# Shifting every weight tile against the moving rows by 192 bytes, reordering the last sums, and moving one start-up load, in a fused attention and mixture-of-experts kernel

## The chip, the cores and the metric

The kernel runs on one core of a Trainium2 chip. Five engines work beside each other: TensorE (PE; its weight loads are listed as PEld), VectorE (DVE), ScalarE (ACT), GpSimd (POOL) and SyncE (SP), with sixteen DMA engines. The metric is the time of one execution on the device in microseconds (us). The kernel before takes 800.86 us, the median of 3 runs (800.49 to 801.48).

## The reference

Attention with a tanh cap, then a top-1 mixture of experts on its output. All data is float32.

```python
# attention: batch 8, 12 heads, 448 tokens, head size 64
scores = cap * tanh((q @ k.T / 8) / cap)
attn = exp(scores - max); attn /= attn.sum(-1) + 1e-9
x = (attn @ v) as 3584 tokens of 768
# experts: 8 of them, 768 -> 1024 -> 768
e = argmax(x @ w_gate)                   # one expert for each token
gate = softmax(x @ w_gate)[e]
out[token] = gate * (relu(x[token] @ w1[e]) @ w2[e])
```

## The kernel before, in words

The attention half takes the 8 images one after the other, in 24 "quads" of four heads, 7 tiles of 64 keys each. A step `k` (84 of them, `STEPS`) handles two tiles: PE makes the scores (L246), ACT applies tanh (L259) and exp (L262), PE multiplies by the values (L312), DVE sums the exponentials for the softmax denominators (`adds`, `fold`, L267). The order is written out by hand: a table `tasks`, filled with `at(step, when, f, ...)`, places the rest of the work (gating, transposes, first loads of experts) in a step, behind its scores on ACT (`"act"`), behind its value products on PE (`"pe1"`) or behind its sums on DVE (`"v"`).

For each image the gating chain is: `strips0` and `strips` (PE: sums over keys and gate logits, L341 to L352), `rec_t` and `rec_v` (DVE: transposes, reciprocal, L367 to L382), `rec_p` and `log_p` (PE, L392 and L408), `route_v` (DVE: argmax, giving `ob`, L434 to L440), `route_s` and `route_g` (gate weight), `place_p` (PE: running counts, L465 and L467), `place_v` (DVE: slots, L477 to L486), and `place_d` (POOL: token lists by DMA). `turn` (L330) transposes one pair of heads' output into the token rows `yt`. The last two images (6 and 7) finish their chains while PE already works on the first block of tokens of an expert.

The expert half works in blocks of tokens of one expert. A large block has 448 tokens, a small one 256. The blocks are run in the order: a first block (`j = -2`) made of tokens of the first images, a second (`-1`), five large ones, two small ones. A block is 8 chunks `f` of the hidden size. `up` (L918) makes hidden rows from 18 matmuls: 6 slices of the input by 3 products. `down` (L948 for large, L956 for small blocks) multiplies them by the second matrix: 18 matmuls of 448 columns, or 12 of 384. Float32 accuracy comes from splitting each operand in a high and a low part (`h` and `l`), hence the three products. The split of the weights is a cast on ACT (L789) and a subtraction on DVE (L794), that of the input L893 and L897.

In `up` the weights that PE holds are `w1` chunks and the rows that stream past them (the moving rows) are `xh`, `xl`. In a large `down` the weights are `w2` chunks and the moving rows the hidden tile `hb` (`hx` and a `kr` buffer in the first block). In a small `down` the roles are exchanged: `hb` is held and `w2` moves. Every matmul is preceded by its own weight load (128 columns of 4 bytes), which PE does while the matmul before it is still streaming.

Where these tiles lie in a partition, in the program as built before: `xh`, `xl`, `hb`, `hx`, the `kr` and `qr` buffers (which serve as chunks 0 and 1 of `w1`), all other `w1` chunks and chunk 0 of `w2` start at 128 modulo 256 bytes. Chunks 1 to 7 of `w2` start at 224. Slices within a tile are multiples of 256 bytes. So, taking the weights that are loaded next against the rows that stream meanwhile, the distance is 0 modulo 256 in every `up`, and in chunk 0 of `down`; it is 96 in chunks 1 to 7 of a large `down`, and 160 in those of a small one.

The start: twenty warm-up matmuls on zeros (L202), while the first keys and queries are loaded by SP (L167, L171), ACT (L168) and POOL (L169).

Of the kernel before, what the change touches and what calls it, by code (L numbers as in the profile page):

```python
# [4 lines left out]
F32 = mybir.dt.float32  # L5
# [96 lines left out]
    return c  # L102


class Pools:


# [16 lines left out]
def attention_moe(tc, qT, kT, vL, capd, wgL, w1a, w1b, w2a, w2b, cst, cmk, out):  # L124
# [31 lines left out]
    def load(mq, part):  # L156

        b, i = divmod(mq, NQ)
        p = slice(2 * i, 2 * i + 2)
        if part == 0:  # L160
            qr = raw.tile([128, 2, S], F32, name="qr")
            kr = raw.tile([128, 2, S], F32, name="kr")
            raws[mq] = qr, kr, pb.tile([128, KT, 2, D], F32, name="vr", bufs=3)
        qr, kr, vr = raws[mq]
        if mq == 0:
            if part == 0:
                nc.sync.dma_start(out=kr[:, :, 0:128], in_=kT[b, :, p, 0:128])  # L167
                nc.scalar.dma_start(out=qr[:, 0], in_=qT[b, :, 0])  # L168
                nc.gpsimd.dma_start(out=qr[:, 1], in_=qT[b, :, 1])  # L169
                nc.scalar.dma_start(out=capt, in_=capd)  # L170
                nc.sync.dma_start(out=kr[:, :, 128:S], in_=kT[b, :, p, 128:S])  # L171
            else:
                nc.sync.dma_start(out=vr, in_=vL[b, :, i])
        elif part == 0:
            nc.sync.dma_start(out=kr, in_=kT[b, :, p])
            nc.sync.dma_start(out=qr, in_=qT[b, :, p])
        else:
            nc.sync.dma_start(out=vr, in_=vL[b, :, i])
# [119 lines left out]
    def fold(m):  # L298
        add(p4s[m], accs[m][:, 0], accs[m][:, 1])
# [438 lines left out]
    def large(j):  # L738
        return j < NL
# [41 lines left out]

    w1s, w2s = [None] * FC, [None] * FC

    def chunk(pool, name):
        return [pool.tile([128, DM], F32R, name=name + i) for i in "hl"]

# [17 lines left out]
    def spare(name):  # L804
        return raw.tile([128, 2, S], F32, name=name).rearrange("p a b -> p (a b)").bitcast(F32R)

    def first_w1(f):
        w1s[f] = [spare(name)[:, 0:DM] for name in ("qr", "kr")]
        split_w1(f)

    idt, gts = {}, {}
# [195 lines left out]
    def at(step, when, f, *a):  # L1007
        tasks.setdefault((step, when), []).append((f, a))

    def do(step, when):  # L1010
        for f, a in tasks.pop((step, when), []):
            f(*a)

    for b in range(B):

        n = (KT * (b * NQ + NQ) - 1) // 2
        at(n + 1, "pe1", strips0, b)
        if b == B - 1:
            continue
        at(n + 4, "v", turn, b * NP + 4)  # L1020
        at(n + 5, "v", turn, b * NP + 5)
        d = n + 5
        at(d, "pe1", strips, b)
        at(d + 1, "v", rec_t, b)
        early = b < B - 2
        p = d + 4 if early else d + 5
        at(d + 2 if early else d + 4, "v", rec_v, b)
        at(p, "pe1", rec_p, b)
        at(p, "pe1", log_p, b)
        at(p + 1, "v", rec_c, b)  # L1030
        at(p + 1, "v", route_v, b)
        at(p + 2, "act", route_s, b)
        at(p + 2, "v", store, b, G)
        at(p + 2, "v", route_g, b)
        at(p + 3, "pe1", place_p, b)
        at(p + 4, "v", place_v, b)
        for q in range(4):
            at(p + 5 + q // 2 * early, "v", place_d, b, q)
    for i in range(QUADS):
        if i % NQ != NQ - 1:  # L1040
            n = (KT * (i + 1) - 1) // 2
            for c in range(2):
                at(n + 4 + c, "v", turn, 2 * i + c)

    n_first = (KT * B_FIRST * NQ - 1) // 2 + 14
    at(0, "v", constants)
# [23 lines left out]
    for k in range(STEPS + 3):  # L1070
        live = k < STEPS
        for n in range(QUADS - 3):
            if k == (KT * (n + 1) - 1) // 2 + 1:
                load(n + 3, 0)
            if k == (KT * (n + 1) - 1) // 2 + 4:
                load(n + 3, 1)
        if live:
            for t in (2 * k, 2 * k + 1):
                scores(t)
                tanh(t)  # L1080
        do(k, "act")
        if 1 <= k <= STEPS:
            expo(k - 1)
        if k == STEPS:
            pools.close("ps_s")
            m["ps_h"] = pools("ps_h", bufs=2, space=PSUM, side="right", **tw)
            m["ps_z"] = pools("ps_z", space=PSUM, side="right", **tw)
            m["h0"] = spare("kr")
            up(-2, 0)
        last = None  # L1090
        if k >= 3:
            ready = held + [2 * k - 6, 2 * k - 5]
            held = [ready.pop()] if ready[-2] % KT == KT - 1 else []
            for t in ready:
                pv(t)
                if t % KT == KT - 1:
                    last = t // KT
        if last is not None:
            outp(last)
        do(k, "pe1")  # L1100
        if 2 <= k < STEPS + 2:
            adds(k - 2)
        do(k, "v")
    fold(QUADS - 1)
    for k in range(STEPS + 3, STEPS + 5):
        do(k, "v")

    pools.close("pb")
    hw = pools("hw", side="right", **tw)
    m["hb"] = hw.tile([128, 6 * LARGE], F32R, name="hb")  # L1110
    for f in range(2, FC):
        w1s[f] = chunk(hw, f"w1{f}")
    w2s[0] = chunk(hw, "w20")
    m["hx"] = pools("hx", side="right", **tw).tile([128, 8 * LARGE], F32R, name="hx")
    assert not tasks and not held
    b = B - 1
    split_w1(2)
    up(-2, 1)
    split_w1(3)
    strips(b)  # L1120
    rec_t(b)
    second_block()
    load_ids(-1)
    load_w(-1, 0, [0])
# [9 lines left out]
    route_v(b)  # L1134
    route_s(b)
    up(-2, 4)
    place_p(b)
    split_w1(6)
    route_g(b)
    place_v(b)  # L1140
    for q in range(4):
        place_d(b, q)
    rec_c(b)
    turn(b * NP + 4)
    turn(b * NP + 5)
    store(b, nc.sync)
    split_w1(7)
    up(-2, 5)
    split_w2(0)
    pools.close("op", "yp", "att")  # L1150
    wb = pools("wb", **tw)
    for f in range(1, FC):
        w2s[f] = chunk(wb, f"w2{f}")
    up(-2, 6)
# [51 lines left out]
    for i, j in enumerate(blocks):  # L1206
# [16 lines left out]
        for f in range(FC):  # L1223
            if 0 < f:
                splits_after(n0, f)
                if n0 == -2 and f == FC // 2 - 1:
                    load_w(n1, 1)
                    put(n0)
            if n1 is not None:
                splits_in(j, f)  # L1230

            down(j, f, range(2) if n1 is not None or f < 3 else range(1))
            if f + 2 < FC:
                if f + 2 == FC - 1 and n1 is not None:
                    scale_x(n1)
                    for k in range(XT):
                        trans_x(n1, k)
                up(j, f + 2)
            if f + 2 == FC and n1 is not None:
                split_xs(n1)  # L1240
                if n2 is not None and not large(n1):
                    make_idx(n2)
                    load_x(n2)
            if f == 4 and n2 is not None:
                load_ids(n2)
                load_w(n2, 0)
# [111 lines left out]
```

## Time and profile before

| what | us |
|---|---|
| median of 3 runs | 800.86 |
| profiled execution | 801.69 |
| span of its instructions | 799.6 |
| PE busy | 782.5 (98%) |
| DVE busy | 549.1 (69%) |
| ACT busy | 452.6 (57%) |
| POOL busy | 362.6 (45%) |

A busy share says only that some instruction was open. Matmuls overlap in the records, each lasting longer than the distance to the next, so how fast PE goes is read from the starts: the distance between two starts is what one matmul costs. In the timeline rows the first number is the start in us from the first instruction, the second the time covered, then engine, line, operation, the tiles written and read, shapes and count, and in brackets the idle time of the engine before it with what ended it. The clock granted to TensorE is at 0.9 of full speed or above in 39 of the page's 40 slices, and at 0.8 in the last.

### The profile page before, as it was taken

The numbers are of one execution on the slowest core, as the hardware profiler recorded it, in microseconds if no ns is written. First come the engines' busy times: TensorE is split into PE (matmuls) and PEld (weight loads), VectorE is DVE, ScalarE is ACT, GpSimd is POOL, SyncE is SP. The second block draws the span as 40 slices with busy tenths as digits, with TensorE's granted clock in tenths as the row PEclk, the third lists the DMA queues.
The fourth block names the chain that finished last, engine by engine and source line by source line (L and its number), as shares of the span: only waits on it lengthen the run. The fifth ranks groups of instructions, "written<-read, shape, count | busy, mean of one in ns | idle before, by whom it ended". The sixth has DMA issues, their size and how long they took to land.

```text
span 799.6 us, 14371 instructions
## 1 busy us (share of the span) xinstructions
PE 782.5 (98%) x5740; PEld 568.2 (71%) x5740; DVE 549.1 (69%) x943; ACT 452.6 (57%) x537; POOL 362.6 (45%) x324
## 2 busy tenths in 40 slices
PE   8999999999999999999999999999999999999996
PEld 3334343444444435889999999999999999999995
DVE  1778988999899998797558358357357367367720
ACT  6999999999999992344334224324333233234421
POOL 1000412135841303671774773773773773747601
PEclk9999999999999999999999999999999999999998
DMA  7243654568988503324264524625520226453301
GB/s 275 88 140 100 180 172 144 169 131 295 238 250 190 156 2 73 82 64 158 60 214 184 214 70 174 218 70 185 208 71 5 72 70 234 155 192 119 143 37 38
DMA packets 34939, 112.76 MB, mean 141 GB/s; under 512 B 8422, under 2 KB 14744, under 8 KB 31792
## 3 DMA queue, kind: packets, MB, share of 16 engines
q0 software_dynamic: 19216, 70.45, 26.7%
q1 hardware_dynamic: 15360, 41.09, 17.0%
q8 instruction: 47, 0.77, 0.4%
q10 hardware_dynamic: 288, 0.23, 0.1%
q14 instruction: 28, 0.23, 0.1%
HBM read 101.87 MB, written 22.85 MB: 156 GB/s over the span
## 4 chain that ended last, share of the span: by engine, by line
PE 77%; ACT 7%; DVE 6%; issue 4%; DMA 3%; POOL 1%; POOLq 0%; SPq 0%; DVEq 0%; ACTq 0%
PE ph L918 27%; PE y L948 22%; PE sp L246 10%; PE po L312 10%; PE y L956 4%; ACT pt L259 3%; ACT pt L262 3%; DVE acc L267 2%; DMA kr<-in_kT 1%; PE ms L349 1%; PE po L948 1%; PE ms L948 1%; DVE p L267 1%; PE z L948 1%; DMA xd<-w2r 1%
## 5 line engine op out<-in xcount | busy, mean ns | idle before, releaser
L928 ACT ACTIVATE hb<-ph 128x448 fp32r<-128x448 f32 (+1 forms) x67 | 34.0, 507 | 265.8 <-PE ph L918 265.8
L749 POOL DMA_INDIRECT xg<-xd,xi x114 | 132.1, 1159 | 58.5 <-issue 35.9
L929 DVE SCALAR_TENSOR_TENSOR hb<-ph,hb 128x448 fp32r<-128x448 f32 (+1 forms) x67 | 38.4, 573 | 170.7 <-ACT hb L928 170.1
L262 ACT ACTIVATE pt<-pt,capt 128x1792 f32<-128x1792 f32 x84 | 153.5, 1829 | 0.0
L246 PE MATMUL sp<-qr,kr 64*64 64x448 f32 x1344 | 149.6, 551 | 3.5 <-ACT pt L259 3.2
L259 ACT ACTIVATE pt<-sp 128x896 f32<-128x896 f32 x161 | 141.1, 947 | 7.8 <-PE sp L246 7.5
L312 PE MATMUL po<-pt,vr 64*64 64x448 f32 x1344 | 144.9, 537 | 0.1
L759 POOL DMA_INDIRECT out<-ys,xi x98 | 107.2, 1093 | 29.9 <-issue 26.5
L246 PEld LDWEIGHTS sp<-qr,kr 64*64 64x64 f32 x1344 | 48.3, 134 | 86.7 <-issue 44.5
L312 PEld LDWEIGHTS po<-pt,vr 64*64 64x64 f32 x1344 | 56.1, 133 | 72.4 <-issue 61.7
L492 POOL DMA_INDIRECT ids<-tokg,slots x32 | 44.4, 1387 | 57.8 <-DVE slots L486 40.1
L267 DVE TENSOR_TENSOR acc<-acc,pt 128x1792 f32<-128x1792 f32 (+1 forms) x36 | 61.2, 1700 | 2.6 <-ACT pt L262 2.5
L267 DVE TENSOR_TENSOR acc<-pt 128x896 f32<-128x896 f32 (+1 forms) x36 | 50.1, 1391 | 5.4 <-ACT pt L262 5.4
L460 POOL DMA_DIRECT2D xd<-w2r x12 | 8.2, 694 | 97.4 <-DVE w2r L397 97.4
L893 ACT CAST xh<-xt 128x448 fp32r<-128x448 f32 (+1 forms) x54 | 27.3, 533 | 27.8 <-DVE xt L889 27.8
L319 DVE COPY ot<-po 128x448 f32<-128x448 f32 x48 | 27.6, 616 | 20.9 <-PE po L312 20.8
L460 POOL DMA_DIRECT2D xd<-yt x16 | 10.5, 664 | 63.4 <-DVE yt L397 63.4
L918 PE MATMUL ph<-xl,qr 128*128 128x448 f32 (+1 forms) x108 | 37.9, 351 | 0.5 <-DVE xl L897 0.5
L918 PE MATMUL ph<-xh,qr 128*128 128x448 f32 (+1 forms) x108 | 37.6, 348 | 0.0
L918 PE MATMUL ph<-xh,kr 128*128 128x448 f32 (+1 forms) x108 | 37.4, 347 | 0.0
L749 POOL DMA_INDIRECT w1r<-in_w1b,widx x7 | 10.3, 1468 | 55.8 <-DVE w17l L794 55.5
L889 DVE STREAM_TRANSPOSE xt<-xg 128x448 f32<-128x448 f32 (+1 forms) x54 | 30.3, 583 | 0.8
(396 smaller groups left out, 1814.6 us busy)
## 6 DMA issues: line engine op xcount, KB each, us to landing
vr<-in_vL SPq DMA_DIRECT2D x24, 448.0 KB, 3.5
kr<-in_kT SPq DMA_DIRECT2D x23, 448.0 KB, 4.8
qr<-in_qT SPq DMA_DIRECT2D x23, 448.0 KB, 6.1
xd<-yt POOLq DMA_DIRECT2D x16, 346.5 KB
xd<-w2r POOLq DMA_DIRECT2D x12, 346.5 KB
xg<-xd,xi POOLq DMA_INDIRECT x114
out<-ys,xi POOLq DMA_INDIRECT x98
w1r<-in_w1a SPq DMA_DIRECT2D x4, 384.0 KB, 4.9
```

What stands on the lines that cost most here:

```text
L246: PE.matmul(sp[w, r, 0:S], kr[h, c, 64 * g : 64 * g + 64], qr[h, c, :], start=True, stop=True)
L259: A.activation(out=pts[t // 2][:, t % 2], in_=sps.pop(t)[:, :, 0:S], func=AF.Tanh, scale=qsc if t < KT else 1.0)
L262: A.activation(out=pts[k], in_=pts[k], func=AF.Exp, scale=capt)
L267: V.tensor_tensor(out=o, in0=a, in1=b, op=ALU.add)
L312: PE.matmul(pvs[m][c][w, 0:S], vr[r, g, j, :], pt[r, j, :], start=g == 0, stop=g == KT - 1)
L492: i = G.indirect_dma_start(out=ids, out_offset=bass.IndirectOffsetOnAxis(ap=slots[0:p, c : c + 1].bitcast(U32), axis=0), in_=tokg[0:p, c, ...
L749: G.indirect_dma_start(out=dst, out_offset=None, in_=src, in_offset=bass.IndirectOffsetOnAxis(ap=idx.bitcast(U32), axis=0), bounds_check=b ...
L759: i = G.indirect_dma_start(out=dst, out_offset=bass.IndirectOffsetOnAxis(ap=idx.bitcast(U32), axis=0), in_=src, in_offset=None, bounds_che ...
L918: PE.matmul(ph, w[:, 128 * k : 128 * k + 128], x[:, k, 0:n], start=i == 0, stop=i == 3 * KC - 1)
L928: A.activation(out=hh, in_=ph, func=AF.Relu)
L929: V.scalar_tensor_tensor(out=hl, in0=ph, scalar=0.0, in1=hh, op0=ALU.max, op1=ALU.subtract)
L948: PE.matmul(y[k][:, 0:LARGE], w[:, c], h, start=f == 0 and i == 0, stop=f == FC - 1 and i == 2)
```

## The change

Four things. First, placement: three padding tiles of 192, 64 and 96 bytes go into the pools that hold `hb`, the `w1` and `w2` chunks, and chunks 0 and 1 of `w1` begin 48 floats into their buffers. As built, all `w1` and `w2` chunks then start at 64 modulo 256, and all of `xh`, `xl`, `hb`, `hx` at 128: the weights loaded next stand at 192 modulo 256 from the moving rows in every `up` and every large `down`. In a small `down` the distance is 64. Second, the order of the last sums, gates and transposes. Third, in small blocks the scaling, transposing and splitting of the next block's input comes one chunk earlier. Fourth, the second half of the first queries is loaded by SP instead of POOL.

```diff
+PADS = (192, 64, 96)
...
-                nc.gpsimd.dma_start(out=qr[:, 1], in_=qT[b, :, 1])
+                nc.sync.dma_start(out=qr[:, 1], in_=qT[b, :, 1])
...
+    def pad(pool, n):
+        pads.append(pool.tile([128, n // 4], F32, name=f"pad{len(pads)}"))
...
-        w1s[f] = [spare(name)[:, 0:DM] for name in ("qr", "kr")]
+        w1s[f] = [spare(name)[:, 48 : 48 + DM] for name in ("qr", "kr")]
...
-        at(d + 2 if early else d + 4, "v", rec_v, b)
+        at(d + 2 if early else d + 3, "v", rec_v, b)
...
-        at(p + 2, "v", route_g, b)
+        at(p + 2 if early else STEPS + 4, "v", route_g, b)
...
-                at(n + 4 + c, "v", turn, 2 * i + c)
+                at(n + 4 + c if i < QUADS - 2 else STEPS + 5, "v", turn, 2 * i + c)
...
+        if k == STEPS + 1:
+            fold(QUADS - 1)
         do(k, "v")
-    fold(QUADS - 1)
-    for k in range(STEPS + 3, STEPS + 5):
-        do(k, "v")
+    do(STEPS + 3, "v")
...
     m["hb"] = hw.tile([128, 6 * LARGE], F32R, name="hb")
+    pad(hw, PADS[0])
     for f in range(2, FC):
         w1s[f] = chunk(hw, f"w1{f}")
     w2s[0] = chunk(hw, "w20")
+    pad(hw, PADS[1])
...
     rec_t(b)
+    for k in range(2):
+        do(STEPS + 4 + k, "v")
     second_block()
...
     up(-2, 4)
+    split_w1(6)
+    rec_c(b)
+    turn(b * NP + 4)
+    turn(b * NP + 5)
+    store(b, nc.sync)
+    up(-2, 5)
     place_p(b)
-    split_w1(6)
     route_g(b)
     place_v(b)
     for q in range(4):
         place_d(b, q)
-    rec_c(b)
-    turn(b * NP + 4)
-    turn(b * NP + 5)
-    store(b, nc.sync)
     split_w1(7)
-    up(-2, 5)
     split_w2(0)
...
     wb = pools("wb", **tw)
+    pad(wb, PADS[2])
...
-                if f + 2 == FC - 1 and n1 is not None:
+                if f + 2 == FC - (1 if large(j) else 2) and n1 is not None:
                     scale_x(n1)
...
-            if f + 2 == FC and n1 is not None:
+            if f + 2 == FC - (not large(j)) and n1 is not None:
                 split_xs(n1)
```

On DVE, where image 6's reciprocal stands among the last steps. Before, `rec_v` (L376 to L382) follows a transpose and the sums `p` of quad 22:

```order
L267 TENSOR_TENSOR acc<-acc,pt 128x1792
L330 STREAM_TRANSPOSE yt<-ot 128x14x32
L267 TENSOR_TENSOR p_3043<-acc 128x896
L267 TENSOR_TENSOR p_3043<-p_3043,pt 128x896
L376 COPY st<-st 64x14x2
L377 COPY st<-lt 32x14x4
L379 RECIPROCAL rec<-st 96x56
L382 TENSOR_TENSOR lt<-lt,rec 96x448
```

The same place in the changed kernel (its lines are numbered 3 higher here):

```order
L270 TENSOR_TENSOR acc<-acc,pt 128x1792
L379 COPY st<-st 64x14x2
L380 COPY st<-lt 32x14x4
L382 RECIPROCAL rec<-st 96x56
L385 TENSOR_TENSOR lt<-lt,rec 96x448
L333 STREAM_TRANSPOSE yt<-ot 128x14x32
L270 TENSOR_TENSOR p_3043<-acc 128x896
L270 TENSOR_TENSOR p_3043<-p_3043,pt 128x896
```

The reciprocal moved in front of three instructions. A little later on DVE, between the argmax of image 6 (`ob`) and its slots (`place_v`, L477 on). Before:

```order
L440 TENSOR_TENSOR ob<-tko,cs 128x32
L330 STREAM_TRANSPOSE yt<-ot 128x14x32
L794 TENSOR_TENSOR kr<-w1r_121,qr 128x768
L267 TENSOR_TENSOR acc<-acc,pt 128x1792
L451 TENSOR_REDUCE gt<-ex 128x4
L453 TENSOR_SCALAR gt<-gt 128x4
L455 RECIPROCAL tokg<-gt 128x4
L330 STREAM_TRANSPOSE yt<-ot 128x14x32
L319 COPY ot<-po 128x448 x2
L267 TENSOR_TENSOR p_3180<-acc 128x896
L477 TENSOR_TENSOR pos<-ms,base 128x32
L479 TENSOR_TENSOR base<-base,ms 128x8
```

In the changed kernel:

```order
L443 TENSOR_TENSOR ob<-tko,cs 128x32
L802 TENSOR_TENSOR kr<-w1r_121,qr 128x768
L270 TENSOR_TENSOR acc<-acc,pt 128x1792
L270 TENSOR_TENSOR p_3180<-acc 128x896
L322 COPY ot<-po 128x448 x2
L480 TENSOR_TENSOR pos<-ms,base 128x32
L482 TENSOR_TENSOR base<-base,ms 128x8
```

Two transposes and the three gate instructions are gone from here. They now stand after image 7's `rec_t` and before `second_block` (L541 on). On SP at the very start, before:

```order
L167 DMA kr<-in_kT 128x2x128
L171 DMA kr<-in_kT 128x2x320
L173 DMA vr<-in_vL 128x896
L175 DMA kr<-in_kT 128x896
L176 DMA qr<-in_qT 128x896
```

And in the changed kernel:

```order
L170 DMA kr<-in_kT 128x2x128
L172 DMA qr<-in_qT 128x448
L174 DMA kr<-in_kT 128x2x320
L176 DMA vr<-in_vL 128x896
L178 DMA kr<-in_kT 128x896
```

The second half of the queries is now SP's second load, in front of the rest of the keys.

## Rows read from the trace of the kernel before

**Rows 1.** Timeline of PE, 381 to 397 us: the first matmul of five chunks.

```profile
381.57 0.36 PE L918 MATMUL ph<-xh,w12h 128*128 128x448 f32 x1
...
385.21 0.56 PE L948 MATMUL y<-hb,w21h 128*128 128x448 f32 x2
...
388.81 0.37 PE L918 MATMUL ph<-xh,w13h 128*128 128x448 f32 x1
...
392.47 0.57 PE L948 MATMUL y<-hb,w22h 128*128 128x448 f32 x2
...
396.18 0.36 PE L918 MATMUL ph<-xh,w14h 128*128 128x448 f32 x1
```

**Rows 2.** Timeline of PE: first matmul of block -1, then of small-block chunks.

```profile
370.63 0.36 PE L918 MATMUL ph<-xh,qr 128*128 128x448 f32 x1
...
721.59 0.28 PE L918 MATMUL ph<-xh,qr 128*128 128x256 f32 x1
...
725.90 0.34 PE L956 MATMUL y<-w20h,hb 128*128 128x384 f32 x1
...
727.99 0.28 PE L918 MATMUL ph<-xh,w12h 128*128 128x256 f32 x1
...
730.13 0.34 PE L956 MATMUL y<-w21h,hb 128*128 128x384 f32 x1
...
732.25 0.28 PE L918 MATMUL ph<-xh,w13h 128*128 128x256 f32 x1
```

**Rows 3.** Timeline of all engines, the first 16 us (SPq is SP's DMA queue).

```profile
0.74 0.46 SPq L167 DMA_DIRECT2D kr<-in_kT  x1
...
1.32 0.74 POOL L169 DMA_DIRECT2D qr<-in_qT  x1 [0.86 <-POOLq L1347]
...
5.44 8.88 PE L246 MATMUL sp<-qr,kr 64*64 64x448 f32 x48
...
6.85 0.37 PEld L246 LDWEIGHTS sp<-qr,kr 64*64 64x64 f32 x8 [1.13 <-DMA qr<-in_qT]
...
8.68 1.01 ACT L259 ACTIVATE pt<-sp,qsc 128x896 f32<-128x896 f32 x1 [5.50 <-PE sp L246]
```

**Rows 4.** Waits of ACT, 8.6 to 302: total us, times, longest us.

```profile
ACT pt L259 <- PE sp L246: 13.5, 17, 5.5
```

**Rows 5.** Waits of PE, 300 to 799: total us, times, longest us.

```profile
PE ms L349 <- DVE pos L481: 1.4, 1, 1.4
PE ms L465 <- DVE ob L440: 0.8, 1, 0.8
PE z L948 <- DVE w22l L794: 0.6, 1, 0.6
PE ph L918 <- DVE xl L897: 0.5, 3, 0.2
```

**Rows 6.** Timeline of PE: the `rec_p` of image 6 and of image 7.

```profile
297.19 0.88 PE L392 MATMUL ms<-rec,cs 96*128 96x56 f32 x6 [1.26 <-DVE rec L379]
...
323.20 0.77 PE L392 MATMUL ms<-rec,cs 96*128 96x56 f32 x6
```

**Rows 7.** Timeline of DVE, 309 to 327 us.

```profile
310.56 0.18 DVE L451 TENSOR_REDUCE gt<-ex 128x4 f32<-128x32 f32 x1
...
311.60 1.12 DVE L319 COPY ot<-po 128x448 f32<-128x448 f32 x2
...
313.85 0.16 DVE L479 TENSOR_TENSOR base<-base,ms 128x8 f32<-128x8 f32 x1
...
321.93 0.50 DVE L379 RECIPROCAL rec<-st 96x56 f32<-96x56 f32 x1
...
326.62 0.23 DVE L832 TENSOR_SCALAR xi<-idt,kc 128x14 int32<-128x14 int32 x1 [2.01 <-DMA idt<-ids,t1i]
```

**Rows 8.** Timeline of PE at the start of the last block: the first and the thirteenth matmul.

```profile
755.88 0.28 PE L918 MATMUL ph<-xh,qr 128*128 128x256 f32 x1
...
758.83 0.28 PE L918 MATMUL ph<-xh,qr 128*128 128x256 f32 x1
```

More of the change, by code (lines that the diff above doesn't have):

```diff
@@ L782, in attention_moe @@
     w1s, w2s = [None] * FC, [None] * FC
+    pads = []
+    def pad(pool, n):
+        pads.append(pool.tile([128, n // 4], F32, name=f"pad{len(pads)}"))
     def chunk(pool, name):
@@ L1113, in attention_moe @@
     w2s[0] = chunk(hw, "w20")
+    pad(hw, PADS[1])
     m["hx"] = pools("hx", side="right", **tw).tile([128, 8 * LARGE], F32R, name="hx")
-    assert not tasks and not held
+    assert not held
     b = B - 1
@@ L1121, in attention_moe @@
     rec_t(b)
+    for k in range(2):
+        do(STEPS + 4 + k, "v")
+    assert not tasks
     second_block()
```

## The prediction

> **What bounds the kernel now.** I read the timeline of PE first, then the waits, then the stretches where PE waits. In the expert half PE alone is the bound: from 370 to 751 us it waits for nothing, and in all of 300 to 799 us only four kinds of wait are listed, 3.3 us together [rows 5]. So there the time is the number of matmuls times the distance between their starts, and the reader is to look at starts, not at durations. Chunk `w12` of `up` begins at 381.57, `w21` of `down` at 385.21, `w13` at 388.81, `w22` at 392.47, `w14` at 396.18 [rows 1]. Each chunk is 18 matmuls of 448 columns, so one costs 3.64/18 = 202.2 ns, 3.60/18 = 200.0, 3.66/18 = 203.3 and 3.71/18 = 206.1. The same instruction with the same shape has three prices. The two `down` chunks have the same distance of 96 between next weights and moving rows, yet one runs at 200 and one at 206: there are two rhythms at one placement. All six blocks from 370.63 to 721.59 [rows 2] repeat this: 350.96/6 = 58.49 us a block, which is 8 `up` chunks at 3.65, `w20` at 3.65 (distance 0, like `up`), `w21`, `w23`, `w25` at 3.60 and four chunks at 3.71 (29.2 + 3.65 + 10.8 + 14.84 = 58.49).
>
> What part of a price streams and what part is a fixed cost? In small blocks 36 `up` matmuls of 256 columns take 721.59 to 725.90, 119.7 ns each, at distance 0; 12 of 384 columns take 725.90 to 727.99, 174.2 at distance 0, and 730.13 to 732.25, 176.7, at 160 [rows 2]. From 256 columns at 119.7 to 448 at 200.0 is 0.418 ns a column, one column per cycle at the full 2.4 GHz. Streaming 448 columns is then some 187 ns; about 13 ns are paid at each of the three widths in its best rhythm, and the worse rhythms add 3 to 7 ns.
>
> The attention half is a chain of ACT and PE. From 8.6 to 302 us ACT waits 13.5 us, always for scores, 5.5 of it before its first tanh [rows 4]: what starts earlier at the head should move the whole half.
>
> **Part 1, placement.** It adds no instruction. Every `up` and large `down` pair goes to distance 192, which no row shows. I bound it by the nearest rows: below by streaming alone, 187 ns, above by twice the fixed part, 213 ns, which allows a loss. I take 200.0, the price of `w21`, for two reasons: it is the lowest price that lasts through a whole chunk, and it lies on the same line of 13 ns plus columns as the 256 and 384 column matmuls at distance 0, so it looks like a rhythm in which nothing collides. It is also the row nearest to the middle of the bounds. In each of six blocks 16 chunks at 3.60 make 57.6 against 58.49: 0.89, or 5.3 us in all. The first block has 8 `up` chunks and `w20` at 3.65, and seven `down` chunks that I take at the slow 3.71: 9 x 0.05 + 7 x 0.11 = 1.2. Sum 6.5 us for 7 x 16 x 18 = 2016 matmuls, whose mean price now is 203.2 ns. The small `down` goes from 160 (and 0) to 64; at 174.2 for its 14 chunks at 160 it gains 14 x 12 x 2.5 ns = 0.4. The faster PE finds DVE, ACT and POOL with room: none of them holds PE up for 380 us.
>
> The Trainium skill, page "TensorE: Matmul & The Clock Gate", section "Part 2: What happens when you issue a matmul", says that PE reads moving rows and next weights through two independent ports, so that loading weights takes nothing from the running matmul. By that rule the distance is without effect and the gain of this part is nothing; that is the first rival. The trace is against it so far, with 200.0 and 206.1 for one shape [rows 1]. Its section "Back-to-back issue gap" gives columns/2.4 + 2.5, which is 189 ns for 448 columns; by that estimate from the page the gain would be 28 us.
>
> **Part 2, the start.** PE's first matmul of scores begins at 5.44, right behind the warm-up; the weight load of the next head pair waits until 6.85 for the queries asked for by POOL at 1.32, and ACT's first tanh begins at 8.68 [rows 3]. Now SP asks for them second, about half a microsecond after its first load at 0.74. The four matmuls of the first tile can then go together, at best at 5.44: 1.4 us earlier. I take 1.1, since the load shares the DMA engines with the two loads in front of it. It costs the later keys one place in SP's queue; they are needed for the third tile only and hide behind the first two. Bounds: 1.4, and a loss of 0.3 if those keys come late.
>
> **Part 3, last sums, gates, transposes.** Four places.
> - `rec_p` of image 6 waits 1.26 us for the reciprocal at 297.19 [rows 6]. In front of that reciprocal stood a transpose and two sums of twice its columns, which it now precedes; three gate instructions and one such transpose alone take 1.04 us [rows 7], so with the sums it is more than is missing, and the wait goes. What is late next is the first `up`, whose PSUM banks are those of the last scores, read by ACT until about the time it would start, and then ACT's relu behind the last exp. I take 0.75 of it (0.3 to 1.26).
> - `strips` of image 7 waits 1.4 us for `place_v` of image 6 [rows 5], whose second instruction is at 313.85. In front of it go the gates and a transpose, 310.56 to 311.60, 1.04 us [rows 7], and another such transpose further up, about half of that again: 1.5 us, so the wait goes. But the same instructions now stand between `rec_t` and `second_block`, so DVE reaches image 7's reciprocal no earlier than now relative to its own start: it ends at 321.93 + 0.50 = 322.43, and PE asked at 323.20 [rows 6, 7]. Of the 1.4 only that slack of 0.77 can be kept. I take 0.55, as a cast on ACT is now waited for.
> - `place_p` of image 7 waits 0.8 us for `ob` [rows 5] with `up` of chunk 5 queued behind it. It moves behind that `up`; cover 3.65 us. What is late next is `w15l`, which follows on DVE the wait of 2.01 us for token numbers that ends at 326.62 [rows 7]; DVE is no earlier there than it reaches `second_block`, which bounds the three gains together. I keep 0.8.
> - `store` of image 7 and its queue (SP) come earlier, the four `place_d` on POOL about as late as now, and the first block that needs those tokens is far behind. The wait for `w22l`, 0.6 [rows 5], stays: DVE there follows PE's sixth `up` and both come earlier together.
>
> Sum 0.75 + 0.55 + 0.8 = 2.1 us; bounds 0.8 and 3.0.
>
> **Part 4, small blocks.** The last block's first 12 distances take 755.88 to 758.83 = 2.95 us [rows 8], where 12 x 119.7 ns = 1.44 would do: 1.5 us lost to input splits that come late. They now come a chunk pair (4 us) earlier, which covers it. I take 1.5; bounds 0.8 and 1.6.
>
> **Sum.** 6.5 + 0.4 + 1.1 + 2.1 + 1.5 = 11.6 us, from the profiled execution's 801.69 (its span of 799.6 and 2.1 around it): 790.1. That execution lies 0.8 above the median of the runs, so a median of 789.3 is my forecast.
>
> **Rivals.**
> *A. Placement does nothing, or does as well as badly* (the mean stays 203.2; the page's two ports would make it so). What is left is 1.1 + 2.1 + 1.5 = 4.7: 796. For it: `up` at distance 0 and the mean `down` at 96 differ by little. Against it: three prices for one shape.
> *B. Distance 192 makes most pairs collide.* Its place is every one of 2016 matmuls; its price is the slow rhythm or one step worse. The change loses from (203.2 x 2016 + 4700)/2016 = 205.5 ns on. At 206.1 it is 803 in terms of the profile; one more step of 3.4 ns, 209.5, gives 801.7 - 4.7 + 12.7 = 810. For it: at one placement both rhythms last for whole chunks [rows 1], so a slow one can lock in. Against it: 192 is a whole number of 64 bytes where 96 is not, and the slow rhythm has only been seen at 96.
> *C. The 13 ns are themselves collisions, and some go.* One step of 3.4 ns below 200 is 196.6: 790.1 - 6.9 = 783; two steps, 193.2: 776; all of it 187: 764. For it: nothing in the trace says that 13 ns must be. Against it: it is the same at three widths and two distances.
> *D. The orders gain nothing*, since the next wait takes their place; 2.1 + 1.1 less: 793. It goes with any of the others.
>
> **How the numbers follow.** Forecast (198 to 201.5 ns) 50%, C 23%, A (201.5 to 204.5) 17%, B 10%. The range should leave out 2 in 10: upward B, downward the further half of C (below 195 ns), so it goes from 780 to 799, the upper end being A with D. A difference within 0.2% (1.6 us) is what a measurement of this kernel can't tell from none; it needs a price near 205.5, or A with all other parts failing: 4%. Slower by more than that: B beyond 206.5 or so: 8%. Faster: 88%.
>
> **What would show it.** In the changed profile: `up` and `down` chunks of the large blocks all 3.60 us apart, without the alternation, a block 57.6 us (A: 58.5; B: over 59.2; C: 56.6 or less); first tanh at about 7.5; no wait of PE for the reciprocal at image 6, none for `place_v`, none for `ob`; the first 12 distances of the last block 1.44 us. The forecast is wrong if large blocks take over 58.2 us or under 57.0, or if attention ends as late as now although the first tanh came earlier.

## The result and the profile after the change

The changed kernel takes 791.89 us in the median of 6 runs (790.94 to 792.99), the kernel before 801.17 beside it (6 runs): ratio 0.9881, interval 0.9860 to 0.9902. That is 9.3 us less; the forecast was 789.3. Its profiled execution took 792.4 us with a span of 790.1, so 9.5 us of span went away.

The large blocks. Timeline of PE, changed kernel: the first matmul of block -1, of the five chunks that [rows 1] shows, and of the first small block.

```profile
369.12 0.36 PE L926 MATMUL ph<-xh,qr 128*128 128x448 f32 x1
...
379.92 0.36 PE L926 MATMUL ph<-xh,w12h 128*128 128x448 f32 x1
...
383.52 0.56 PE L956 MATMUL y<-hb,w21h 128*128 128x448 f32 x2
...
387.12 0.36 PE L926 MATMUL ph<-xh,w13h 128*128 128x448 f32 x1
...
390.72 0.56 PE L956 MATMUL y<-hb,w22h 128*128 128x448 f32 x2
...
394.32 0.36 PE L926 MATMUL ph<-xh,w14h 128*128 128x448 f32 x1
...
714.72 0.28 PE L926 MATMUL ph<-xh,qr 128*128 128x256 f32 x1
```

Each chunk is 3.60 us, with no alternation; six blocks take 714.72 - 369.12 = 345.60 us, 57.60 each, where [rows 2] had 350.96. That is 5.36 us.

The start. Timeline of all engines, changed kernel, first 14 us.

```profile
1.26 0.45 SPq L172 DMA_DIRECT2D qr<-in_qT  x1
...
7.17 1.90 ACT L262 ACTIVATE pt<-sp,qsc 128x896 f32<-128x896 f32 x2 [3.99 <-PE sp L249]
...
13.81 1.88 PE L249 MATMUL sp<-qr,kr 64*64 64x448 f32 x16 [1.59 <-ACT pt L262]
```

The first tanh is 1.51 us earlier than in [rows 3], and two tanh now run back to back (x2). The first exp comes at 11.08 us, in the kernel before at 13.19, and PE's fourth batch of scores 2.1 us earlier (13.81, before 15.92). Attention keeps that: `rec_p` of image 6 starts at 293.69 without a wait, 3.5 us before that of [rows 6], and the first `up` at 294.97, 3.4 earlier (298.38 in the kernel before).

The end of attention. Waits of PE, 16 us to the end: total us, times, longest us.

```profile
PE ph L926 <- DVE w15l L802: 2.0, 1, 2.0
...
PE ms L395 <- DVE rec L382: 0.8, 1, 0.8
PE z L956 <- DVE w22l L802: 0.7, 1, 0.7
PE ms L352 <- DVE pos L484: 0.3, 1, 0.3
```

Of [rows 5] the wait for `ob` and those for `xl` are gone and that for `pos` has shrunk. The first row is new, and there is more behind it. Here are DVE, POOL and PE in the timeline of the changed kernel, 313 to 332 us.

```profile
313.62 0.18 DVE L458 RECIPROCAL tokg<-gt 128x4 f32<-128x4 f32 x1
...
325.82 0.23 DVE L840 TENSOR_SCALAR xi<-idt,kc 128x14 int32<-128x14 int32 x1 [4.37 <-DMA idt<-ids,t1i]
325.97 0.95 DVE L802 TENSOR_TENSOR w15l<-w1r,w15h 128x768 fp32r<-128x768 f32 x1
...
314.33 1.02 POOL L495 DMA_INDIRECT ids<-tokg,slots  x1 [8.98 <-DVE tokg L458]
...
323.24 1.05 POOL L752 DMA_INDIRECT idt<-ids,t1i  x1 [4.07 <-issue]
...
326.97 0.47 PE L926 MATMUL ph<-xh,w15l 128*128 128x448 f32 x1 [1.98 <-DVE w15l L802]
...
327.48 0.46 PE L926 MATMUL ph<-xl,w15h 128*128 128x448 f32 x1
...
331.07 0.36 PE L926 MATMUL ph<-xh,w15l 128*128 128x448 f32 x1
```

In the kernel before the first of the four scatters of image 6 stood so in the timeline of POOL:

```profile
315.06 1.25 POOL L492 DMA_INDIRECT ids<-tokg,slots  x1 [6.36 <-DVE slots L486]
```

Read it from the first PE row upward. PE waits for `w15l` (326.97), which on DVE stands behind `xi`, which waits 4.37 us for the token numbers of the second block, which POOL asks for at 323.24, when image 6's four scatters into the same table are through; they began at 314.33, behind `tokg`, the last of the three gate instructions of image 6. In the kernel before the gates ran at 310.56 [rows 7], and the scatters waited for the slots and not for them. PE is now 3.4 to 4.7 us earlier, but the gates are 2.7 us later (the first of them at 313.24), so the scatters begin only 0.7 us earlier than before and the gather behind them 1.0 (it was at 324.22). What PE's clock did behind this wait stands in the busy times by stretch of the same kernel (us, then busy us and instructions of PE, PEld, DVE, ACT, POOL; granted clock; DMA share; GB/s).

```profile
326.00:328.00 2.00, 1.03 (x4) 0.95 (x5) 1.83 (x8) 0.64 (x2) 1.46 (x1) 0.90 0.03 0
328.00:330.00 2.00, 2.00 (x7) 1.73 (x7) 1.87 (x4) 0.86 (x2) 1.61 (x2) 0.50 0.36 86
```

After 1.98 us of waiting PE ran at the lower level in 328 to 330 (0.50, 1.2 GHz), though it worked without a pause there. The ten distances from 327.48 to 331.07 in the timeline take 3.59 us where 2.00 would do at 200 ns: the lower clock cost 1.6 us. Timeline of PE, the first `up` and the first `down`, changed kernel and then the kernel before:

```profile
294.97 0.47 PE L926 MATMUL ph<-xh,qr 128*128 128x448 f32 x1
...
339.30 0.36 PE L956 MATMUL z<-kr,w20h 128*128 128x448 f32 x1
```
```profile
298.38 0.47 PE L918 MATMUL ph<-xh,qr 128*128 128x448 f32 x1
...
340.15 0.57 PE L948 MATMUL z<-kr,w20h 128*128 128x448 f32 x2
```

It is 44.33 us from one to the other, 2.56 more than before.

The small blocks. Timeline of PE at the start of the last block, changed kernel.

```profile
748.34 0.28 PE L926 MATMUL ph<-xh,qr 128*128 128x256 f32 x1
...
749.75 0.28 PE L926 MATMUL ph<-xh,qr 128*128 128x256 f32 x1
```

Twelve distances take 1.41 us, where [rows 8] had 2.95. All small blocks and the end together, from 714.72 to 790.1, take 75.38 us for 78.01.

The account, by starts on PE: head of attention and `rec_p` -3.41, first `up` to first `down` +2.56, seven `down` of the first block with their `w20` -0.66, six large blocks -5.36, small blocks and end -2.63: -9.50, the difference of the spans.

### The profile page after: what moved, and what is told of

It reads as the page before. It is cut to its first block, busy times and chain, and to the rows that moved or that the text cites. A ratio compares the mean times of both kernels' runs of the same rounds, so it can differ in the third digit from the quotient of the medians.

```text
span 790.1 us, 14368 instructions
## 1 busy us (share of the span) xinstructions
PE 773.5 (98%) x5740; PEld 568.0 (72%) x5740; DVE 548.3 (69%) x943; ACT 452.0 (57%) x537; POOL 363.6 (46%) x323
## 4 chain that ended last, share of the span: by engine, by line
PE 56%; DVE 1%; issue 1%; DMA 0%; POOL 0%; ACT 0%; POOLq 0%; DVEq 0%
PE ph L926 27%; PE y L956 22%; PE y L964 4%; PE ms L956 1%; PE po L956 1%; PE z L956 1%; DMA idt<-ids,t1i 0%; DVE w21l L802 0%; DVE w22l L802 0%; POOL ids L495 0%; DVE w15l L802 0%; DVE first L680 0%; ACT w21h L797 0%; POOL out L762 0%; ACT hx L936 0%
## 5 line engine op out<-in xcount | busy, mean ns | idle before, releaser
L249 PE MATMUL sp<-qr,kr 64*64 64x448 f32 x1344 | 147.2, 547 | 3.8 <-ACT pt L262 3.7
```

The lines of the kernel that those rows point to most:

```text
L249: PE.matmul(sp[w, r, 0:S], kr[h, c, 64 * g : 64 * g + 64], qr[h, c, :], start=True, stop=True)
```

## The experiments

In the runs e1 to e4 and e9 to e12 PE also stood at many other places, up to 5.5 us at one, for weights, for hidden rows and for no releaser that the profile shows, and the kernel before took 849 and 893 us beside them; so of these runs only undisturbed stretches of the trace are read, and their times say nothing.

**e1_no_place: the changed kernel without Part 1.**

```
-    def pad(pool, n):
-        pads.append(pool.tile([128, n // 4], F32, name=f"pad{len(pads)}"))
+    def pad(pool, n):
+        pads.append(n)
...
-        w1s[f] = [spare(name)[:, 48 : 48 + DM] for name in ("qr", "kr")]
+        w1s[f] = [spare(name)[:, 0:DM] for name in ("qr", "kr")]
```

> The changed kernel with Part 1 taken out: no filler tiles, first two chunks of w1 back at the start of their tiles, so that the distances are again 0 for `up` and 0 or 96 for `down`; all orders stay as changed. Theory (the distance alone sets the price of an expert matmul): the large blocks go back to the two rhythms, 58.5 us each against 57.60, 6 x 0.89 = 5.3 us; the first block gives back about 0.6, the 256-column matmuls of the small blocks 119.7 for 117.6 ns, 1.0 us. Time 791.9 + 6.9 = 798.8 us. Rival (the matmuls got faster because PE comes to these blocks earlier or by the changed orders, not by the addresses): blocks of 57.6, time 792. What is left between 798.8 and the 801.2 of the kernel before is what the orders and the start are worth together: 2.4 us.

Measured 841.8 us beside 849.4. Timeline of PE: four chunk starts of block -1, and the start of the next block.

```profile
390.68 0.57 PE L956 MATMUL y<-hb,w21h 128*128 128x448 f32 x2
...
394.28 0.37 PE L926 MATMUL ph<-xh,w13h 128*128 128x448 f32 x1
...
397.93 0.37 PE L956 MATMUL y<-hb,w22h 128*128 128x448 f32 x1
...
401.64 0.36 PE L926 MATMUL ph<-xh,w14h 128*128 128x448 f32 x1
...
434.59 0.36 PE L926 MATMUL ph<-xh,qr 128*128 128x448 f32 x1
```

3.60, 3.65 and 3.71 us are back, with all orders as changed; the block (376.08 to 434.59) takes 58.51 us. The orders have no part in the price. They do make the loss behind attention: first `up` to first `down` is 44.31 us here, where e2, with the placement alone, has 41.34, and PE waits 1.81 us for `w15l`, with the lower clock behind it.

**e2_place_alone: the kernel before with all of Part 1 and nothing else.**

```
+PADS = (192, 64, 96)
...
-        w1s[f] = [spare(name)[:, 0:DM] for name in ("qr", "kr")]
+        w1s[f] = [spare(name)[:, 48 : 48 + DM] for name in ("qr", "kr")]
...
+    pad(hw, PADS[0])
...
+    pad(hw, PADS[1])
...
+    pad(wb, PADS[2])
```

> The kernel before with Part 1 alone: all filler tiles, the first two chunks of w1 192 bytes into their tiles, no order moved, queries as before. Theory: every large chunk 3.60 us, six large blocks 345.6 us for 351.0, first block 0.6 less, small blocks 1.0 less by the 256-column matmuls; the input splits in the last block are still late. Time 801.2 - 6.9 = 794.3 us. Rival (part of the gain needs the orders): 797 or more.

Measured 827.1 us beside 849.4. Timeline of PE, starts of block -1 and of the next:

```profile
379.37 0.36 PE L926 MATMUL ph<-xh,qr 128*128 128x448 f32 x1
...
436.96 0.36 PE L926 MATMUL ph<-xh,qr 128*128 128x448 f32 x1
```

57.59 us. Placement alone gives the whole price, and with e1 this is shown from both sides.

**e3_gates_early, and again as e5_gates_early_again: the gates of image 6 at once behind its slots.**

```
-        at(p + 2 if early else STEPS + 4, "v", route_g, b)
         at(p + 3, "pe1", place_p, b)
         at(p + 4, "v", place_v, b)
+        at(p + 2 if early else STEPS + 3, "v", route_g, b)
```

> The changed kernel with one line moved: the three gate instructions of image 6 follow its slots at once (before the split of w12), not behind image 7's transposes of the logits. Theory (PE's new wait of 1.98 us at 326.97 for w15l comes from a chain: gates of image 6 at 313.6, its four scatters on POOL from 314.3 on, the gather of the second block's token numbers that waits for them to land, 325.8, `xi` on DVE in front of the split of w15; and the clock at 0.60 of full in 327 to 330 us follows from PE's idle time): the scatters start some 3.3 us earlier, `xi` stands at about 322.5, PE no longer waits at w15l and its clock stays at 1.00 there, so 2.0 + 1.7 = 3.7 us go: 788.2 us. Rival 1 (the scatters are held by something else, such as the store of image 6's tokens in the same queue): no change, 792. Rival 2 (the next wait comes at once, at w16l or at ob, or the strips of image 7 lose what is won): 790 to 791.

> The same kernel as e3_gates_early (gates of image 6 at once behind its slots), whose time could not be read: on that chip PE stood for 1 to 2 us at the same chunks of every block and the kernel before took 849 us. Its stretch from the first `up` to the first `down` had already shrunk from 44.3 us in the changed kernel to 40.5. Theory: nothing behind takes these 3.8 us back, so 788.1 us and a ratio of 0.9837 to the kernel before. Rival (what follows, the weights of the second half of the first block, comes no earlier, so that the wait for w22l grows from 0.7 to as much as 4 us): 791 to 792.

e3: 815.6 us beside 849.4; no wait of PE for `w15l`, and 40.50 us from the first `up` to the first `down`. e5: 789.04 us (4 runs, 788.55 to 789.43), ratio to before 0.9849, 0.9830 to 0.9868. Timeline of DVE, POOL and PE of e5:

```profile
311.24 0.18 DVE L458 RECIPROCAL tokg<-gt 128x4 f32<-128x4 f32 x1
...
324.10 0.23 DVE L840 TENSOR_SCALAR xi<-idt,kc 128x14 int32<-128x14 int32 x1 [1.71 <-DMA idt<-ids,t1i]
...
320.75 2.03 POOL L752 DMA_INDIRECT idt<-ids,t1i  x1 [3.71 <-DVE rec L382]
...
325.75 0.36 PE L926 MATMUL ph<-xh,w15l 128*128 128x448 f32 x1
```

The token numbers land early enough, PE passes at 200 ns, and its granted clock is 1.00 in each stretch from 325 to 335 us. First `up` to first `down`: 295.92 to 336.39, 40.47 us, 3.86 less than in the changed kernel; the wait for `w22l` stays 0.7. The median fell by 2.9 us and not 3.9; in the profiled execution 0.9 of the difference is a wait of ACT at 259.43 us (0.92, for `df`, L449) that the edit doesn't touch. The theory holds, and the rivals fall.

**e4_ids_late: `make_idx(-1)` and `load_x(-1)` behind the split of w15.**

```
-    make_idx(-1)
-    load_x(-1)
     rec_p(b)
     log_p(b)
     split_w1(5)
+    make_idx(-1)
+    load_x(-1)
```

> The changed kernel with two calls moved: the second block's token indices (`xi`) and the gathers that use them come behind the split of w15 in DVE's order instead of in front of it; the gates stay as changed. Theory (w15l is late only because it is queued behind `xi`, which waits for the landing of the token numbers): w15l is done at about 322, PE passes without the 1.98 us of wait and at a clock of 1.00; the waiting `xi` now holds up the choice of experts of image 7 and the split of w16, needed at about 328.4 and ready near 328.9: a wait of 0.3 to 0.6 us there. Time 791.9 - 3.3 = 788.6 us. Rival (w15l waits for PE's or ACT's side, for instance the cast of w15h): PE waits as long as now, 792.

Measured 821.2 us beside 849.4. Two rows of the timeline of PE:

```profile
331.13 0.36 PE L926 MATMUL ph<-xh,w15l 128*128 128x448 f32 x1
...
335.68 0.18 PE L468 MATMUL ms<-ob,mk 128*128 128x40 bf16 x1 [1.18 <-DVE yt L400]
```

`w15l` is no longer waited for, so its place behind `xi` was the cause; a wait turns up at `place_p`, of 1.2 us where I expected 0.3 to 0.6, since what DVE does behind `xi`, down to the copy L400 that the row names, now comes late. First `up` to first `down`: 41.82 us, 2.5 better than changed and 1.3 worse than e3.

**e6, e7, e8, e12: other distances, the same for `up` and `down`.** All change the three filler sizes and the offset of the first chunks, as here for 64:

```
-PADS = (192, 64, 96)
+PADS = (64, 192, 224)
...
-        w1s[f] = [spare(name)[:, 48 : 48 + DM] for name in ("qr", "kr")]
+        w1s[f] = [spare(name)[:, 16 : 16 + DM] for name in ("qr", "kr")]
```

> The changed kernel with all distances of the large matmuls at 64 bytes instead of 192 (small `down` at 192 instead of 64). Theory 1 (only the distances 0 and 96 collide in part; any other whole number of 64 bytes is alike): 200.0 ns a matmul, 791.9 us. Theory 2 (what counts is that next weights lie in the last quarter of 256 bytes behind the moving rows): 64 runs at another price, 196.6 or 203 to 207 ns; 2016 matmuls x 3.4 ns = 7 us either way, 785 or 799.

> The changed kernel with all distances at 128 bytes, half a period of 256 (small `down` at 128 too). Theory 1 (only 0 and 96 collide): 200.0 ns, 791.9 us. Theory 2 (the collision falls off with the distance to the next multiple of 256, so 128 is the best): under 200 ns, at one step of 3.4 ns 785 us. Theory 3 (the period is 128, not 256): as at distance 0, 202.7 ns with starts of 200 to 207 ns mixed, 791.9 + 2016 x 2.7 ns + 1.0 for the small blocks = 798.3 us.

> The changed kernel with all distances at 96 bytes, `up` as well as `down` (small `down` at 160). In the kernel before only `down` had 96, between `up` chunks at 0, and ran chunk by chunk at 200.0 or 206.7 ns. Theory 1 (the rhythm is set by the phase in which the first matmul of a chunk falls, and 96 itself holds both): one rhythm locks in for the whole block; if it is the slow one, 2016 x 6.7 ns = 13.5 us more, 805; if the fast one, 792. Theory 2 (the slow rhythm is that of a distance that is not a whole number of 64 bytes): 206.7 ns throughout, 805 us. Rival (the mix of distances, not 96, made the slow chunks): 200.0 ns throughout, 792 us.

> The changed kernel with all distances at 160 bytes (small `down` at 96). So far 0 gives 202.7 ns, 64 202.3, 96 200.0, 128 204.0, 192 200.0. Theory 1 (a symmetry about 128: 64 and 192 would then be alike, which they are not, so this one is nearly out; it says 160 as 96): 200.0 ns, 791.9 us, or 790 if PE's wait for w15l stays short enough to leave the clock at 1.00. Theory 2 (bad are the distances that one of two accesses, 64 bytes apart, brings to a common place: 0 and 64, 128): 160 is like 96 and 192, 200.0 ns. Theory 3 (a distance is the worse the nearer it lies to 128, with 96 an exception): 202 to 204 ns, 796 to 800 us. For 384 columns at 96: 173 to 177 ns.

Timelines of PE, starts of block -1 and of the next, at 64, 96, 128 and 160:

```profile
369.30 0.37 PE L926 MATMUL ph<-xh,qr 128*128 128x448 f32 x1
...
427.54 0.37 PE L926 MATMUL ph<-xh,qr 128*128 128x448 f32 x1
```
```profile
366.45 0.36 PE L926 MATMUL ph<-xh,qr 128*128 128x448 f32 x1
...
424.05 0.36 PE L926 MATMUL ph<-xh,qr 128*128 128x448 f32 x1
```
```profile
367.10 0.37 PE L926 MATMUL ph<-xh,qr 128*128 128x448 f32 x1
...
425.85 0.37 PE L926 MATMUL ph<-xh,qr 128*128 128x448 f32 x1
```
```profile
382.59 0.37 PE L926 MATMUL ph<-xh,qr 128*128 128x448 f32 x1
...
441.73 0.37 PE L926 MATMUL ph<-xh,qr 128*128 128x448 f32 x1
```

A block has 288 matmuls. The last column is the mean time between starts of the 384-column `down` matmuls of small blocks at that distance, each from the run in which they have it (178, or 171 at 96).

| distance | block, us | ns per matmul of 448 | time and ratio | ns per matmul of 384 |
|---|---|---|---|---|
| 64 (e6) | 58.24 | 202.2 | 795.34, 0.9924 (0.9900 to 0.9948) | 176.0 |
| 96 (e8) | 57.60 | 200.0 | 790.82, 0.9882 (0.9858 to 0.9906) | 174.2 |
| 128 (e7) | 58.75 | 204.0 | 798.09, 0.9970 (0.9959 to 0.9982) | 175.9 |
| 160 (e12) | 59.14 | 205.3 | 899.1 beside 892.9, not comparable | 177.0 |
| 192 (changed) | 57.60 | 200.0 | 791.89, 0.9881 (0.9860 to 0.9902) | 173.8 |

e6: theory 1 falls, since 64 isn't like 192; theory 2 had the sign of it and not the size. e7: theory 3 has the time (798.3 for 798.09) and still falls, since with a period of 128 the distances 64 and 192 would be one. That its time fits is luck: the price is 204.0 and not 202.7, and first `up` to first `down` is 1.91 us shorter than in the changed kernel (42.42), with a wait for `w15l` of 1.42 us and the clock at 1.00. e8: with 96 for every chunk the rhythm of 206 ns occurs in no chunk of the six blocks, so theory 2 falls. The rival (alternating with chunks at 0 made the slow ones) fits, but so does the fast branch of theory 1 (one rhythm locks in), and these runs don't tell the two apart. e12: no theory holds; 160 is the worst of all, and not like 96. So neither whole multiples of 64 bytes nor a symmetry about 128 marks a good distance. At 128 the single distances run from 195 to 212 ns, so 200 isn't a floor for one matmul; no mean of a whole chunk under 199.9 was seen. Which accesses collide, these runs don't say; 32 and 224 were not tried.

Two things more can be read from these traces. In all large matmuls the moving rows stay at 128 modulo 256, so the distance and the weights' own place change together there. In small `down` they don't: the held rows are at 128 in e6 and in the changed kernel and at 0 in e9 (below), the moving ones at 192, 64 and 64. The distances are 192, 64 and 192, and the prices 173.8, 176.0 and 173.7 ns. That fits the distance, and neither address by itself. And the order of good and bad isn't the same at each width: distance 0 is among the best for 384 columns (173.9 ns in chunk 0 of the kernel before) and among the worst for the 256 columns of `up` in small blocks (119.5; 117.6 at 64, 118.3 at 96, 118.9 at 128, 120.1 at 160, 117.1 at 192).

e8 is faster than its placement explains: its first `up` to its first `down` is 42.35 us, 1.98 less than in the changed kernel. `w15l` is waited for there too, but 1.55 us, and the clock stays at 1.00: 0.43 us of waiting less, and the 1.6 us of the lower clock. In e6 the wait is 1.78 us and the clock falls. Timeline of PE and busy times by stretch of e8, then of e6:

```profile
326.15 0.47 PE L926 MATMUL ph<-xh,w15l 128*128 128x448 f32 x1 [1.55 <-DVE w15l L802]
```
```profile
326.00:328.00 2.00, 1.85 (x9) 1.76 (x10) 1.77 (x8) 1.46 (x3) 1.70 (x2) 1.00 0.14 36
```
```profile
326.85 0.47 PE L926 MATMUL ph<-xh,w15l 128*128 128x448 f32 x1 [1.78 <-DVE w15l L802]
```
```profile
328.00:330.00 2.00, 2.00 (x6) 1.76 (x6) 1.86 (x5) 0.74 (x2) 1.69 (x2) 0.50 0.34 85
```

**e9_best: the gates early, `rec_v` of image 7 ahead of `second_block`, small hidden rows 128 bytes further.**

```
-            b, s = m["hb"], 2 * n * (f % (3 if n == LARGE else 5))
+            b, s = m["hb"], 2 * n * (f % 3) if n == LARGE else 2 * n * (f % 5) + 32
...
+    rec_v(b)
     second_block()
...
     up(-2, 2)
-    rec_v(b)
```

> The changed kernel with three edits: the gates of image 6 at once behind its slots (as in e5), `rec_v` of image 7 in front of `second_block` on DVE, and the hidden rows of small blocks 128 bytes further into `hb`, which puts their `down` at distance 192 instead of 64. Theory: the first edit is worth 2.9 us as measured in e5; the second removes PE's wait of 0.8 us for the reciprocal; the third brings the 384-column matmuls of small blocks from 176.4 to 173.5 ns, as they ran at 192 in e6, 768 x 2.5 ns = 1.9 us. Time 791.9 - 2.9 - 0.8 - 1.9 = 786.3 us. Rival 1 (PE merely waits elsewhere: the token numbers of the second block are asked for 1.4 us later on DVE's side, so `xi` and w15l come late again): 787 to 789. Rival 2 (in e6 the 173.5 ns came from `up` at 64 beside it, not from `down` at 192): 788.2 us.

Measured 844.9 us beside 892.9. First `up` to first `down`: 304.52 to 344.93, 40.41 us, where e5 has 40.47: the reciprocal is no longer waited for, but the stretch is hardly shorter, and PE waits 0.55 us for hidden rows in front of chunk `w14` instead. Rival 1 has the outcome, that PE merely waits elsewhere, but not the place: `xi` and `w15l` aren't waited for by PE. The 384-column matmuls run at 173.7 ns, so rival 2 falls. But I had counted 768 of them, and the trace has two small blocks with 96 each (the others stand in code that this execution doesn't enter), so the edit is worth 192 x 2.3 ns = 0.4 us, less than a measurement can tell. So the best version with a time that can be read is e5.

**e10_start_alone: the kernel before with the queries asked for by SP.**

```
-                nc.gpsimd.dma_start(out=qr[:, 1], in_=qT[b, :, 1])
+                nc.sync.dma_start(out=qr[:, 1], in_=qT[b, :, 1])
```

> The kernel before with one edit of the change: the second half of the first queries is asked for by SP, second in its queue, not by POOL. Theory (the head of ACT's chain moves the whole attention half, since ACT hardly waits after it): first tanh at 7.2 instead of 8.7, first exp at 11.1 instead of 13.2, the last large block starts 2.1 us earlier: 801.0 - 2.1 = 798.9 us. Rival (the waits at the end of attention, for the reciprocal and the slots, take it back): first exp at 11.1, time 800.5 or more.

Measured 879.3 us beside 892.9, not comparable. Its head is early (first exp at 10.45 us against 13.19 in the kernel before, 11.08 in the changed one; 0.42 of it because its scores begin at 5.02 and not at 5.44). The waits of PE at the end of attention don't take it back, as the rival has it: they are 1.3 (reciprocal), 1.4 (slots) and 0.6 us (`ob`), for 1.3, 1.4 and 0.8 in the kernel before, and first `up` to first `down` is 41.57 us for 41.77. What it gives to the whole time can't be read in this run.

**e11_splits_late: the input splits of small blocks at their old place.**

```
-                if f + 2 == FC - (1 if large(j) else 2) and n1 is not None:
+                if f + 2 == FC - 1 and n1 is not None:
...
-            if f + 2 == FC - (not large(j)) and n1 is not None:
+            if f + 2 == FC and n1 is not None:
```

> The changed kernel with the input splits of small blocks back at their old place, one chunk pair later; everything else as changed. Theory (the 1.5 us that the first matmuls of the last block lost were waits for these splits): they are back, 793.4 us, with distances of 240 ns and more at the start of the last block. Rival (with the placement and the start changed, DVE comes early enough anyway): 792, all distances of that block near 118.

Measured 858.3 us beside 892.9. Timeline of PE at the start of the last block:

```profile
805.97 0.28 PE L926 MATMUL ph<-xh,qr 128*128 128x256 f32 x1
...
807.37 0.38 PE L926 MATMUL ph<-xl,qr 128*128 128x256 f32 x1 [0.16 <-DVE xl L905]
...
809.28 0.28 PE L926 MATMUL ph<-xh,qr 128*128 128x256 f32 x1
```

Twelve distances take 3.31 us for 1.41, with PE waiting for `xl`; some 0.5 of it comes with a late `w25l` of this run. The waits for the splits are back, as the theory has it.

## Why the prediction was right, and where it was wrong

**Placement: right, for a reason that was half wrong.** 6.5 was forecast for the large matmuls; the six blocks gave 5.36 (forecast 5.3), and the first block's `down` with `w20` 0.66 of a forecast 0.82. Its `up` lie in the stretch where a wait and a lower clock cover them, so their 0.4 can't be read. The price of 200.0 held, and the runs undo most of what it was taken from. No row of the kernel before has 448 columns at 64, 128, 160 or 192, and the first three cost 202.2 to 205.3, so that 200.0 came true at this distance is in part luck. The second reason, one line of 13 ns plus columns through three widths as the rhythm in which nothing collides, falls: at 192 the 256-column matmuls take 117.1 ns, 2.4 less than at 0, and are no longer on that line. The argument against rival B, that 192 is a whole number of 64 bytes, falls with e6 and e7. Rival A and rival B were real dangers: at 64 A would have come true (202.2), at 160 nearly B (205.3, the point from which the change loses being 205.5). Two smaller terms were off: the small `down` at 64 gained nothing (176.0 ns, 175.9 before) where I had 0.4, and the 256-column matmuls, for which I had nothing, went from 119.5 to 117.1 ns, 288 x 2.4 ns = 0.7.

The Trainium skill, page "TensorE: Matmul & The Clock Gate", section "Part 2: What happens when you issue a matmul", has moving rows and next weights read through two independent ports, so that loading weights takes no read bandwidth from the running matmul. By that rule no distance between them would matter; the measurement decides against it here, with 200.0 to 205.3 ns for one instruction by address alone. The formula in the section "Back-to-back issue gap" of the same page of the Trainium skill, which that section gives for single matmuls apart from a stream of weight loads and matmuls, makes 189 ns of 448 columns; the lowest mean of a chunk in these runs is 199.9.

**Start: the term was mis-sized.** Forecast 1.1 with a bound of 1.4, measured 2.1. The first tanh came 1.51 us earlier, so the load lost nothing by sharing the DMA engines, where I had taken 0.3 off; and from the first tanh to the first exp it is 3.91 us where it was 4.51, since the tanh now come in pairs: another 0.6 that I had not counted at all. e10 shows the early head with this load alone.

**Last sums, gates, transposes: the step failed.** Its three gains came. The wait at image 6's `rec_p` went whole (1.3 us for a forecast 0.75), the wait for `place_v` fell from 1.4 to 0.3, and that for `ob` went. Of the second I had said that only the slack in front of the reciprocal can be kept, and PE does wait 0.83 us there now. But the sentence that failed is "DVE is no earlier there than it reaches `second_block`, which bounds the three gains together. I keep 0.8". It took `xi`'s wait of [rows 7] for one that moves with DVE. It hangs on the scatters of image 6, these on the gates, and the change moves the gates of image 6 behind `rec_t` of image 7, which I had counted only as DVE time in front of other DVE work, not as the start of a chain through POOL, DMA and DVE to PE. Instead of a gain of 0.55 + 0.8 in this stretch there is a loss of 2.56: 1.98 us of waiting and 1.6 of the lower clock against some 1.0 that was gained ahead of it. e5, which has neither, is 3.86 us shorter there. e5 and e4 show the cause from two sides, the gates and the place of `w15l`; e1 (44.31 us), e2 (41.34) and e10 (41.57) show that it is the orders, and neither the placement nor the earlier start.

**Small blocks: right.** 1.5 forecast, 1.54 measured at the place named, and e11 brings the wait back.

The sum is 2.1 us short of the forecast 11.6: start and `rec_p` 1.6 us better, the stretch behind them 4.3 worse (its `up` at 0.05 a chunk counted), small blocks 0.7 better, the rest 0.1 worse. The wait for `w15l` and the lower clock behind it, 3.6 us together, are more than this difference.

## What to carry to other kernels

When matmuls of one shape have several prices, measure start to start over whole chunks, give all of them one distance between next weights and moving rows, and try several at each width; neither alignment nor symmetry tells which is good. When a step is moved back, follow each thing that it writes to the DMA that reads it and to what stands behind that DMA's waiter on the next engine; the cost is there and not in the step. Here a wait of 1.98 us on TensorE cost another 1.6 us through the clock.

## What was not expected of the hardware

- The pitch of fp32r matmuls with 448 columns goes with the distance between next weights and moving rows, modulo 256 bytes (the rows at 128 in all of them): 202.2 ns at 64, 200.0 at 96, 204.0 at 128, 205.3 at 160, 200.0 at 192, and 202.2 to 203.3 at 0 [rows 1].
- One distance (96) can have two pitches: 200.0 ns throughout when all chunks have it, 200 or 206 chunk by chunk between chunks at 0.
- After waits for `w15l` of 1.98 (changed), 1.81 (e1) and 1.78 us (e6) PE's granted clock fell from 1.00 to 0.50; after 1.73 (e12), 1.67 (e11), 1.55 (e8) and 1.42 us (e7) at the same place it stayed at 1.00. Whether the length of the wait decided it, these runs don't show.
